# Attention and MLP in one kernel: casts placed ahead of their transposes, constants filled by block on VectorE, a rate of MLP work for each block

## The chip, the cores and the metric

The kernel runs on one core of one Trainium2 chip. The metric is the time on the device in microseconds (us), the median of several runs. A ratio is the mean time of one kernel's fast runs over that of the other's of the same rounds, so it is not quite the ratio of the medians that are quoted beside it.

The program fills the instruction queues of five engines: TensorE (PE in the profile; PEld are its weight loads), VectorE (DVE), ScalarE (ACT), GpSimd (POOL) and SyncE (SP, which here issues DMAs). The program lays down the order of each queue. Semaphores order the queues against each other.

## The reference, cut to what matters

```python
# q, k, v: 4 batches x 8 heads x 768 x 64, float32
ub     = sum_d max(q*k_min(chunk), q*k_max(chunk))    # bound for each of 24 chunks of 32 keys
sel    = the 6 chunks of the highest bound (causal)
scores = where(sel & causal, q @ k.T / 8, -1e9)
x      = softmax(scores) @ v                          # -> 3072 tokens x 512
h      = x @ w_in                                     # 512 x 2048
g      = softplus(h)
out    = g @ w_out                                    # 2048 x 512, float32
```

## The kernel before

The tokens are cut into 12 blocks of 256, in the order `00 10 01 11 02 12 20 21 30 31 22 32` (batch, block within the batch). The instructions of all engines are issued in an order that the program lays down itself. Its unit is the *slot*: one score step (two matmuls and one Exp), and after it whatever else the slot has to carry. There are 192 score steps and, after blocks 0 and 1, 12 slots that carry no scores, so 204 slots.

```python
def slot(rate):
    ...                                   # P*V steps and stores that have come due
    credit[0] += rate
    while credit[0] >= 1.0:
        credit[0] -= 1.0
        if next(mlp, "end") == "wait":    # the next x is not ready: the slot has no MLP step
            credit[0] = 0.0
    for g_ in agenda.pop(clock[0], []):   # steps that prepare later blocks
        next(g_, None)
    ...
```

The MLP is a stream of 192 steps. An h step is 8 matmuls of 256 columns and an Exp; every second one adds a Ln. A y step is 4 matmuls of 512 columns. x of a block has to be ready before its first h step.

```python
run_block(0, 0.0)
run_block(1, 0.0)
for _ in range(IDLE):                     # 12 slots of MLP alone
    slot(1.0)
for n in range(2, NB):
    run_block(n, 0.91)                    # 0.91 MLP steps for each slot
```

What is left of the stream after the last score runs alone at the end (the *tail*).

The first three blocks (the *ramp*) are prepared by half: cast to bf16 on ScalarE, transpose on TensorE, copy out of PSUM on ScalarE, in this order for one half of k or q, and only then for the next.

```python
def turn(xf, g):
    xb = half_pool.tile([128, NT, H // 2, D], BF16, name="xb")
    nc.scalar.copy(xb, xf[:, :, 4 * g:4 * g + 4])            # cast
    xT = new_xT()
    for t in range(NT):
        for p in range(2):
            nc.tensor.transpose(xT[:, t, p], xb[:, t, 2 * p:2 * p + 2, :], ident)
    return xT
# ... [cut] then nc.scalar.copy(kth or qt, xT)
```

Constants are written for a whole batch image at once, for two images (i = 0, 1):

```python
def consts(i):
    nc.gpsimd.memset(KB[i][0:32], 0.0)
    nc.vector.tensor_copy(KA[i][64:96], ohb.unsqueeze(1).to_broadcast([32, NP, S]))
    nc.vector.tensor_copy(KB[i][32:64], ohb.unsqueeze(1).to_broadcast([32, NP, S]))
    nc.vector.memset(BD[i], 0.0)
    nc.vector.memset(V[i][:, :, :, D:D + 1], 1.0)
```

Blocks 3 to 11 are prepared in fixed slots on VectorE (`prep_block`): chunk extremes, bounds, MAX8, comparison. The mask of chosen chunks (`mraw`) goes through a DMA transpose (`mt`), is copied into `qa` and `qt`, and the first score of the block waits for it.

The softmax here doesn't subtract the row's maximum and nothing guards it: scores larger than these inputs give would overflow.

Of the kernel before, what the change touches and what calls it, by code (L numbers as in the profile page):

```python
# [11 lines left out]
BF16 = mybir.dt.bfloat16  # L12
# [7 lines left out]
def kernel(  # L20
# [9 lines left out]
    nc = tc.nc  # L30
    B, H, S, D = q.shape
# [4 lines left out]
    NP = H // 2  # L36
# [6 lines left out]
    QB = 256  # L43
    NT = QB // 128
    NBLK = S // QB
    NCB = QB // CH
    order = "00 10 01 11 02 12 20 21 30 31 22 32"
    blocks = [(int(o[0]), int(o[1])) for o in order.split()]
# [12 lines left out]
    half_pool = ctx.enter_context(tc.tile_pool(name="half", bufs=2))  # L61
    pt_pool = ctx.enter_context(tc.tile_pool(name="pt", bufs=5))
    st_pool = ctx.enter_context(tc.tile_pool(name="st", bufs=4))
    x_pool = ctx.enter_context(tc.tile_pool(name="x", bufs=5))
    g_pool = ctx.enter_context(tc.tile_pool(name="g", bufs=3))
    e_pool = ctx.enter_context(tc.tile_pool(name="e", bufs=3))
    mo_pool = ctx.enter_context(tc.tile_pool(name="mo", bufs=3))
# [1 line left out]
    ps_o = ctx.enter_context(tc.tile_pool(name="ps_o", bufs=2, space=PS))  # L69
    ps_t = ctx.enter_context(tc.tile_pool(name="ps_t", bufs=1, space=PS))  # L70
    ps_h = ctx.enter_context(tc.tile_pool(name="ps_h", bufs=2, space=PS))
# [3 lines left out]
    KA = [singles.tile([128, NP, S], BF16, name=f"ka_{i}") for i in range(2)]  # L75
    KB = [singles.tile([128, NP, S], BF16, name=f"kb_{i}") for i in range(2)]
# [50 lines left out]
    ohb = singles.tile([32, S], BF16, name="ohb")  # L127
# [12 lines left out]
    for i in range(2):  # L140
        nc.vector.memset(Mraw[i], 0.0)

    def consts(i):
        nc.gpsimd.memset(KB[i][0:32], 0.0)
        nc.vector.tensor_copy(KA[i][64:96], ohb.unsqueeze(1).to_broadcast([32, NP, S]))
        nc.vector.tensor_copy(KB[i][32:64], ohb.unsqueeze(1).to_broadcast([32, NP, S]))
        nc.vector.memset(BD[i], 0.0)
        nc.vector.memset(V[i][:, :, :, D:D + 1], 1.0)

    def load_w_in():  # L150
        for kt_ in range(KDM):
            nc.gpsimd.dma_start(out=w_in_sb[:, kt_], in_=moe_w_in[kt_ * 128:(kt_ + 1) * 128, :])
            yield
# [18 lines left out]
    def spots(n):  # L172
        b, blk = blocks[n]
        return (KA[b % 2], KB[b % 2], BD[b % 2], Mraw[n % 2],
                blk, slice(blk * QB, (blk + 1) * QB))

    def extremes(n, ps, ts, kT):
        bd, blk = spots(n)[2], spots(n)[4]
        npp, ntt = ps.stop - ps.start, ts.stop - ts.start
        c0 = blk * NCB + 4 * ts.start  # L180
        kx = half_pool.tile([128, npp, 2, ntt, 4], BF16, name=f"kx{npp}")
        for m, op in ((0, ALU.max), (1, ALU.min)):
            nc.vector.tensor_reduce(kx[:, :, m].rearrange("d p t c -> d t p c"),
                                    kT.rearrange("d t p (c e) -> d t p c e", e=CH),
                                    axis=AX.X, op=op)
        sh = [128, npp * 2, 2, 4 * ntt]
        nc.vector.tensor_tensor(
            bd[:, ps, :, :, c0:c0 + 4 * ntt].rearrange("d p m h c -> d (p m) h c"),
            kx.rearrange("d p m t c -> d (p m) (t c)").unsqueeze(2).to_broadcast(sh),
            sel.unsqueeze(1).unsqueeze(3).to_broadcast(sh), op=ALU.mult)  # L190
# [29 lines left out]
    def prep_first(n):  # L220
        ka, kb, bd, mraw, blk, cs = spots(n)
        al = slice(0, NT)
        qt = qt_pool.tile([128, NT, NP, 128], BF16, name="qt")
        qa = qt_pool.tile([128, NT, NP, 128], BF16, name="qa")
        Q[n] = (qa, qt)
        kf, qf = xfs.pop(("k", n)), xfs.pop(("q", n))
        H2 = {}

        def new_xT():
            if n < 2:  # L230
                return ps_h.tile([128, NT, 2, 128], BF16, name="xT", tag="hp")
            return ps_t.tile([128, NT, 2, 128], BF16, name="xT", tag="t")

        def turn(xf, g):
            xb = half_pool.tile([128, NT, H // 2, D], BF16, name="xb")
            nc.scalar.copy(xb, xf[:, :, 4 * g:4 * g + 4])  # L236
            xT = new_xT()
            for t in range(NT):
                for p in range(2):
                    nc.tensor.transpose(xT[:, t, p], xb[:, t, 2 * p:2 * p + 2, :], ident)  # L240
            return xT

        def a_k(g):
            kT = turn(kf, g)
            H2["k", g] = kT, half_pool.tile([128, NT, 2, 128], BF16, name="kth")
            nc.scalar.copy(H2["k", g][1], kT)

        def a_q(g):
            qT = turn(qf, g)
            nc.scalar.copy(qt[:, :, 2 * g:2 * g + 2], qT)  # L250

        def b_(g):
            extremes(n, slice(2 * g, 2 * g + 2), al, H2["k", g][0])

        def c_(g):
            ps = slice(2 * g, 2 * g + 2)
            kt = H2["k", g][1]
            qpos = half_pool.tile([128, NT, 2, 128], BF16, name="qph")
            qneg = half_pool.tile([128, NT, 2, 128], BF16, name="qnh")
            nc.vector.tensor_scalar_max(qpos, qt[:, :, ps], 0.0)  # L260
            nc.vector.tensor_scalar_min(qneg, qt[:, :, ps], 0.0)
            H2["q", g] = qpos, qneg
            nc.gpsimd.tensor_copy(ka[0:64, ps, cs].rearrange("d p (t s) -> d p t s", s=128),
                                  kt[0:64].rearrange("d t p s -> d p t s"))
            nc.gpsimd.tensor_copy(qa[0:64, :, ps], qt[0:64, :, ps])
            nc.gpsimd.tensor_copy(kb[64:128, ps, cs].rearrange("d p (t s) -> d p t s", s=128),
                                  kt[64:128].rearrange("d t p s -> d p t s"))

        def d_(g):
            ps = slice(2 * g, 2 * g + 2)  # L270
            qpos, qneg = H2["q", g]
            ub = ps_t.tile([128, NT, 2, 2, NCH], F32, name="ub", tag="t")
            ub_sb = half_pool.tile([128, NT, 2, 2, NCH], F32, name="ub_sbh")
            m8 = half_pool.tile([128, NT, 2, 2, 8], F32, name="m8h")
            bounds(n, ps, al, qpos, qneg, ub, ub_sb, m8)
            choose(n, ps, al, ub_sb, m8)

        def e_(g):
            ps = slice(2 * g, 2 * g + 2)
            mT = ps_t.tile([64, NT, 2, 128], BF16, name="mTh", tag="t")  # L280
            for t in range(NT):
                for p in range(2):
                    nc.tensor.transpose(mT[:, t, p], mraw[:, t, 2 * g + p], ident)  # L283
            nc.vector.tensor_copy(qa[64:96, :, ps], mT[0:32])
            nc.scalar.copy(qt[32:64, :, ps], mT[32:64])

        return {"k": a_k, "q": a_q, "b": b_, "c": c_, "d": d_, "e": e_}

    def put_mask(n, mt):
        qa, qt = Q[n]  # L290
# [179 lines left out]
    def at(slot_no, gen):  # L470
        agenda.setdefault(slot_no, []).append(gen)
# [20 lines left out]
    def run_block(n, rate):  # L492
        assert n in Q
        for p in range(NP):
            for _ in score_step(n, p):
                slot(rate)
# [5 lines left out]
    def do(f, *args):  # L502
        f(*args)
        yield

    def hold(ap):
        nc.gpsimd.tensor_copy(gate, ap)

    def now(gen):
        for _ in gen:  # L510
            pass

    IDLE = 12
    starts = {}
# [14 lines left out]
    for n in range(3, NB):  # L529
# [12 lines left out]
        if n > 3:  # L542
            at(turns[0] - 14, queue(load_cast("k", n), load_cast("q", n)))
            at(max(turns[0] - 6, last_of(n) + 8), queue(load_cast("v", n)))

    consts(0)
    now(load_f32("v", 0, (nc.sync, nc.sync), 1))
    now(load_f32("k", 1, (nc.sync, nc.sync), 1))
# [1 line left out]
    now(load_f32("v", 1, (nc.sync, nc.sync), 1))  # L550
    xfq1 = xfs["q", 1]
    f0 = prep_first(0)
    for st in ("k0", "q0", "k1", "q1", "b0", "c0", "b1", "d0", "c1", "e0"):
        f0[st[0]](int(st[1]))

    def cast_v(n):
        for t in range(NT):
# [2 lines left out]
    f1 = prep_first(1)  # L560
    f2 = {}
# [10 lines left out]

    def stages(f, plan_):
        for slot_, names in plan_:
            for s_ in names.split():
                at(slot_, do(lambda s_=s_: f[s_[0]](int(s_[1]))))

    stages(f0, ((0, "d1"), (1, "e1")))
    at(2, do(cast_v, 0))
    at(3, do(consts, 1))  # L580
    at(4, do(hold, xfq1[0:1, 1, 7, 0:1]))
    at(4, do(lambda: now(load_w_in())))
    stages(f1, ((3, "k0"), (4, "q0"), (5, "b0 k1 q1"), (6, "c0 b1"), (7, "d0 c1 e0"),
                (9, "d1"), (10, "e1")))
    at(10, do(cast_v, 1))
    at(14, do(b2_loads))
    at(20, do(lambda: hold(xfq2[0][0:1, 1, 7, 0:1])))
    at(20, do(lambda: now(load_w_out())))
    at(20, do(lambda: now(load_cast("v", 2))))
    at(20, queue(load_cast("k", 3), load_cast("q", 3), load_cast("v", 3)))  # L590
    stages(f2, ((19, "k0"), (20, "b0"), (21, "q0 c0"), (22, "d0"), (23, "e0 k1"), (24, "b1"),
                (25, "q1 c1"), (26, "d1"), (27, "e1")))
    run_block(0, 0.0)
    run_block(1, 0.0)
    for _ in range(IDLE):
        slot(1.0)
    for n in range(2, NB):
        run_block(n, 0.91)
    while later:
        slot(1.0)  # L600
    clock[0] = NEVER
# [32 lines left out]
```

## Time and profile before

331.24 us, the median of 3 runs (330.64 to 331.49). The profiled run is another one. It took 332.4 us, so spans read from its trace exaggerate by about 1 us.

The first lines of the profile page of before: busy time with its share of the span for each engine, and two rows of the 40 slices (tenths busy of TensorE, and tenths of full speed that its clock was granted).

```profile
span 330.7 us, 6455 instructions
PE 265.0 (80%) x2472; PEld 185.8 (56%) x2472; DVE 162.8 (49%) x571; ACT 216.1 (65%) x371; POOL 112.5 (34%) x189
...
PE   1443594669877989898898699789899999999994
...
PEclk9999999778999799999999799979999999999999
```

The slices are 8.3 us long. TensorE is mostly at 8 or 9 from slice 10 on and mostly between 1 and 6 before. Holes remain (a 6 at slice 23).

The table of stretches of before, cut where the stages change: until the first MLP matmul, the slots of MLP alone, until the last Exp of attention, and the tail. The columns are start and end, length, busy us of PE, PEld, DVE, ACT and POOL with instruction counts, the mean granted clock of TensorE, the DMA share and GB/s. The clock record of these traces begins only near 46 us, so the 1.00 of a first line was not measured.

```profile
0.00:44.00 44.00, 17.65 (x151) 11.84 (x152) 28.49 (x96) 21.45 (x41) 22.06 (x41) 1.00 0.71 126
44.00:74.00 30.00, 19.46 (x148) 13.54 (x149) 9.93 (x38) 17.74 (x27) 16.15 (x23) 0.83 1.31 165
74.00:294.00 220.00, 196.40 (x1964) 141.18 (x1964) 119.69 (x430) 161.13 (x283) 73.86 (x126) 0.97 0.77 88
294.00:331.00 37.00, 31.46 (x214) 19.22 (x212) 4.67 (x8) 15.83 (x22) 0.41 (x1) 0.99 0.13 47
```

No engine is full in the first 74 us: that is a chain. From 74 us on TensorE is 89% busy, and what it leaves idle is 24 us in the long stretch.

What TensorE waited for, in two windows of before, from the view of waits (who waited for whom, us in total, number of waits, longest). First 44 to 74 us, then 74 to 294 us.

```profile
PE xT L240 <- ACT xb L236: 9.5, 4, 2.5
...
PE s_ps L348 <- ACT pt L352: 6.7, 16, 0.9
PE y L428 <- DVE y_sb L433: 5.3, 6, 1.7
PE s_ps L348 <- DVE qa L293: 5.1, 4, 3.1
PE ub L198 <- DVE qpos L308: 2.8, 2, 2.1
```

The first line is four groups of transposes that waited 2.4 us each for a cast. The cast itself takes 0.60 to 0.62 us, but it stands in ScalarE's queue behind Exp and Ln of the MLP, as the timeline of ScalarE in before shows (start, duration, engine, line, operation, tiles; idle time before it in brackets):

```profile
48.91 1.07 ACT L414 ACTIVATE e_sb<-hp 128x512 f32<-128x512 f32 x2
50.01 1.06 ACT L416 ACTIVATE g<-e_sb 128x1024 bf16<-128x1024 f32 x1
50.97 0.60 ACT L236 CAST xb<-two 128x512 bf16<-128x512 f32 x1
```

The timeline of the start of before, VectorE and POOL:

```profile
1.60 3.09 DVE L130 TENSOR_SCALAR ohb<-ident,shift 32x768 bf16<-32x768 bf16 x1
1.63 2.65 POOL L144 MEMSET kb_110<- 32x3072 bf16 x1
...
8.08 0.64 DVE L183 TENSOR_REDUCE kx_199<-xT 128x16 bf16<-128x512 bf16 x1
```

VectorE's instruction, which fills `ohb`, takes 3.09 us for 768 elements per partition. (Some texts below call it the first VectorE operation; two short ones, of 0.18 and 0.14 us, go before it.)

### The profile page before, as it was taken

The page shows a single profiled execution, that of the slowest core. Times are in us where ns is not written, and L with a number is a line of the kernel's source. Part 1 is how long each engine was busy: PE and PEld are TensorE (multiplying, and loading weights), DVE is VectorE, ACT ScalarE, POOL GpSimd, SP SyncE. Part 2 cuts the span into 40 slices and gives each one's busy share as a digit, 9 for nine tenths or more (in the row PEclk, how much of TensorE's full clock was granted, in tenths as well). Part 3 has the DMA queues.
Part 4 walks back from the last instruction along what each step waited for, and adds up shares of the span by engine and source line. Part 5 has one row for each costly group of instructions (what it writes and reads, how often), then busy time and mean ns, then how long its engine had stood idle before and what let it go on. Part 6 is the DMA issues. An engine that isn't in the chain of part 4 may idle for free.

```text
span 330.7 us, 6455 instructions
## 1 busy us (share of the span) xinstructions
PE 265.0 (80%) x2472; PEld 185.8 (56%) x2472; DVE 162.8 (49%) x571; ACT 216.1 (65%) x371; POOL 112.5 (34%) x189
## 2 busy tenths in 40 slices
PE   1443594669877989898898699789899999999994
PEld 0222363436534756765765586567567767776641
DVE  8764622433657548636756957549375211111001
ACT  4454367559534794985794599658787978876540
POOL 5357228545433422404536545732111001000000
PEclk9999999778999799999999799979999999999999
DMA  9908679999999856765999799999211110001101
GB/s 168 212 2 164 123 148 144 179 135 113 102 107 145 95 47 113 93 83 64 163 83 111 130 112 98 113 95 144 64 44 23 49 49 33 18 34 53 60 32 63
DMA packets 118082, 31.48 MB, mean 95 GB/s; under 512 B 112420, under 2 KB 114468, under 8 KB 118052
## 3 DMA queue, kind: packets, MB, share of 16 engines
q0 software_dynamic: 60928, 11.54, 43.9%
q1 hardware_dynamic: 55012, 19.01, 29.0%
q10 hardware_dynamic: 2112, 0.52, 0.9%
q8 instruction: 19, 0.31, 0.4%
q14 instruction: 11, 0.09, 0.1%
HBM read 27.26 MB, written 6.29 MB: 101 GB/s over the span
## 4 chain that ended last, share of the span: by engine, by line
PE 52%; ACT 23%; DVE 15%; DMA 5%; issue 4%; POOL 0%; ACTq 0%; POOLq 0%
PE y L428 19%; PE hp L412 18%; ACT g L416 7%; ACT e_sb L414 7%; ACT pt L352 6%; PE s_ps L348 5%; PE o_ps L373 5%; DMA mt<-mraw_115 4%; PE s_ps L350 3%; DVE y_sb L433 2%; DMA x<-o_sb 2%; ACT xb L236 1%; PE xT L240 1%; PE mTh L283 1%; DVE m8h L207 1%
## 5 line engine op out<-in xcount | busy, mean ns | idle before, releaser
L352 ACT ACTIVATE pt<-s_ps 128x512 bf16<-128x512 f32 (+1 forms) x192 | 99.4, 540 | 45.3 <-PE s_ps L350 44.2
L412 PE MATMUL hp<-x,w_in_sb 128*128 128x256 bf16 x768 | 106.3, 285 | 1.8 <-DMA x<-o_sb 1.5
L428 PE MATMUL y<-w_out_sb,g 128*128 128x512 bf16 x384 | 98.4, 381 | 6.9 <-DVE y_sb L433 6.9
L356 POOL TENSOR_SCALAR_AFFINE_SELECT pt<-pt 128x256 bf16<-128x256 bf16 x96 | 40.5, 423 | 160.2 <-ACT pt L352 159.6
L412 PEld LDWEIGHTS <-w_in_sb 128*128 128x128 bf16 x768 | 75.7, 102 | 16.5 <-issue 2.5
L414 ACT ACTIVATE e_sb<-hp 128x512 f32<-128x512 f32 x96 | 57.3, 598 | 32.7 <-PE hp L412 32.2
L428 PEld LDWEIGHTS <-g 128*128 128x128 bf16 x384 | 34.9, 98 | 34.5 <-issue 8.9
L416 ACT ACTIVATE g<-e_sb 128x1024 bf16<-128x1024 f32 x48 | 50.7, 1057 | 1.5
L379 DVE RECIPROCAL rec<-o_ps 128x4 f32<-128x4 f32 x48 | 8.8, 183 | 79.9 <-PE o_ps L373 79.9
L433 DVE COPY y_sb<-y 128x512 f32<-128x512 f32 x24 | 16.6, 690 | 42.7 <-PE y L428 42.6
L373 PEld LDWEIGHTS <-pt 128*128 128x128 bf16 x672 | 30.1, 102 | 3.3 <-issue 1.2
L240 PE MATMUL xT<-ident,xb 128*128 128x128 bf16 x48 | 6.4, 278 | 24.4 <-ACT xb L236 24.4
L383 DVE TENSOR_TENSOR o_sb<-o_ps,rec 128x256 bf16<-128x256 f32 x48 | 20.4, 424 | 1.7
L240 PEld LDWEIGHTS <-xb 128*128 128x128 bf16 x48 | 3.7, 119 | 27.5 <-ACT xb L236 27.5
L348 PE MATMUL s_ps<-qa,ka_109 96*128 96x256 bf16 x48 | 13.7, 287 | 6.3 <-DVE qa L293 3.6
L373 PE MATMUL o_ps<-v_107,pt 128*128 128x65 bf16 x336 | 17.0, 200 | 1.0 <-ACT v_107 L558 1.0
L348 PE MATMUL s_ps<-qa,ka_108 96*128 96x256 bf16 x48 | 14.1, 295 | 3.5 <-DVE qa L293 1.5
L116 POOL DMA_DIRECT2D k_sb<-in_k_dram x18 | 16.3, 906 | 1.2 <-issue 0.7
L348 PE MATMUL s_ps<-qt,kb_110 128*128 128x256 bf16 x48 | 14.0, 291 | 3.2 <-ACT pt L352 3.0
L116 POOL DMA_DIRECT2D q_sb<-in_q_dram x18 | 16.2, 901 | 0.9 <-issue 0.3
L373 PE MATMUL o_ps<-v_106,pt 128*128 128x65 bf16 x336 | 16.3, 198 | 0.0
L348 PE MATMUL s_ps<-qt,kb_111 128*128 128x256 bf16 x48 | 13.8, 289 | 1.0 <-ACT pt L352 0.7
(190 smaller groups left out, 319.0 us busy)
## 6 DMA issues: line engine op xcount, KB each, us to landing
out_dram<-y_sb SPq DMA_DIRECT2D x24, 256.0 KB, 2.0
k_sb<-in_k_dram POOLq DMA_DIRECT2D x18, 128.0 KB, 4.1
q_sb<-in_q_dram POOLq DMA_DIRECT2D x18, 128.0 KB, 4.6
w_in_sb<-in_moe_w_in_dram POOLq DMA_DIRECT2D x4, 512.0 KB, 8.2
w_out_sb<-in_moe_w_out_dram POOLq DMA_DIRECT2D x4, 512.0 KB, 9.6
v_106<-in_v_dram POOLq DMA_DIRECT2D x10, 128.0 KB, 5.5
v_107<-in_v_dram POOLq DMA_DIRECT2D x10, 128.0 KB, 4.8
two<-in_v_dram SPq DMA_DIRECT2D x4, 256.0 KB, 5.2
```

What stands on the lines that cost most here:

```text
L116: nc.gpsimd.dma_start(out=xb[:, t], in_=rows(nm, n, t))
L240: nc.tensor.transpose(xT[:, t, p], xb[:, t, 2 * p:2 * p + 2, :], ident)
L348: nc.tensor.matmul(s_ps[:, 0:QB], kk[0:nr, p, j * 128:(j + 1) * 128], qq[0:nr, :, p, :], start=True, stop=True)
L352: nc.scalar.activation(pt[:, h, j:j + 2].rearrange("k j c -> k (j c)")[:, 0:w], s_ps[:, 0:w], ACT.Exp, scale=scale)
L356: nc.gpsimd.affine_select(out=diag, in_=diag, compare_op=ALU.is_ge, fill=0.0, base=0, channel_multiplier=-1, pattern=[[0, 2], [1, 128]])
L373: nc.tensor.matmul(o_ps[:, u, h], pt[:, h, j, c0:c0 + 128], V[b % 2][:, j, 2 * p + h, :], start=(j == 0), stop=(j == t0 + u))
L383: nc.vector.tensor_tensor(o_sb[:, :, p % 2], o_ps[:, :, :, 0:D], rec.to_broadcast([128, NT, 2, D]), op=ALU.mult)
L412: nc.tensor.matmul(hp[:, fi], w_in_sb[:, dt, ft * 128:(ft + 1) * 128], X[n][:, dt // 2, :, dt % 2, :], start=(dt == 0), stop=(dt == KDM - 1))
L414: nc.scalar.activation(e_sb[:, f2 * 2:f2 * 2 + 2], hp, ACT.Exp)
L416: nc.scalar.activation(g[:, f4 * 4:(f4 + 1) * 4], e_sb, ACT.Ln, bias=1.0)
L428: nc.tensor.matmul(y, g[:, f, u * 128:(u + 1) * 128], w_out_sb[:, f, :], start=(f == 0), stop=(f == KFF - 1))
L433: nc.vector.tensor_copy(y_sb, y)
```

## The change

The intent has three parts. (1) In the ramp, casts are issued ahead of the transposes that they feed, so that TensorE and ScalarE do not take turns; one q cast of block 0 moves to VectorE, and the q transposes of blocks 0 and 1 go to other PSUM buffers than the k transposes. Loading of w_in is released two slots earlier. (2) The constants are filled for one block at a time, with the zeros on VectorE rather than on POOL. (3) The MLP gets a rate for each block: fewer steps where x is late, one for each slot from block 7 on. The number of x buffers falls from 5 to 4.

```diff
-    x_pool = ctx.enter_context(tc.tile_pool(name="x", bufs=5))
+    x_pool = ctx.enter_context(tc.tile_pool(name="x", bufs=4))
...
-    def consts(i):
-        nc.gpsimd.memset(KB[i][0:32], 0.0)
-        nc.vector.tensor_copy(KA[i][64:96], ohb.unsqueeze(1).to_broadcast([32, NP, S]))
-        nc.vector.tensor_copy(KB[i][32:64], ohb.unsqueeze(1).to_broadcast([32, NP, S]))
+    for i in range(2):
         nc.vector.memset(BD[i], 0.0)
         nc.vector.memset(V[i][:, :, :, D:D + 1], 1.0)
+
+    def consts(n):
+        b, blk = blocks[n]
+        c = slice(blk * QB, (blk + 1) * QB)
+        row = ohb[:, c].unsqueeze(1).to_broadcast([32, NP, QB])
+        nc.vector.tensor_copy(KA[b % 2][64:96, :, c], row)
+        nc.vector.tensor_copy(KB[b % 2][32:64, :, c], row)
+        nc.vector.memset(KB[b % 2][0:32, :, c], 0.0)
...   # turn() and a_k(), a_q() are split into cast (c or v), turn (t) and evac (e)
-    for st in ("k0", "q0", "k1", "q1", "b0", "c0", "b1", "d0", "c1", "e0"):
-        f0[st[0]](int(st[1]))
+    steps(f0, "ck0 vq0 tk0 tq0 ek0 eq0 ck1 cq1 tk1 tq1 b0 c0 ek1 eq1 d0 e0 b1 c1")
...
-    stages(f0, ((0, "d1"), (1, "e1")))
+    stages(f0, ((0, "d1"), (2, "e1")))
...
-    at(4, do(hold, xfq1[0:1, 1, 7, 0:1]))
-    at(4, do(lambda: now(load_w_in())))
-    stages(f1, ((3, "k0"), (4, "q0"), (5, "b0 k1 q1"), (6, "c0 b1"), (7, "d0 c1 e0"),
-                (9, "d1"), (10, "e1")))
-    at(10, do(cast_v, 1))
+    at(2, do(hold, xfq1[0:1, 1, 7, 0:1]))
+    at(2, do(lambda: now(load_w_in())))
+    stages(f1, ((3, "ck0 cq0 tk0 tq0 ek0 eq0"), (5, "ck1 cq1 b0 tk1 tq1"), (6, "c0 ek1 eq1 d0 b1"),
+                (7, "e0 c1 d1"), (9, "e1")))
+    at(9, do(cast_v, 1))
...
+    at(18, do(consts, 2))
...
-    stages(f2, ((19, "k0"), (20, "b0"), (21, "q0 c0"), (22, "d0"), (23, "e0 k1"), (24, "b1"),
-                (25, "q1 c1"), (26, "d1"), (27, "e1")))
+    stages(f2, ((19, "ck0 tk0 ek0"), (20, "b0 cq0"), (21, "tq0 eq0 c0"), (22, "d0"), (23, "e0 ck1 tk1 ek1"),
+                (24, "b1 cq1"), (25, "tq1 eq1 c1"), (26, "d1"), (27, "e1")))
+    for n in range(3, 2 * NBLK):
+        at(starts[n] - 6, do(consts, n))
...
-        run_block(n, 0.91)
+        run_block(n, {2: 0.4, 3: 0.55, 4: 0.85, 5: 0.65, 6: 0.7}.get(n, 1.0))
```

## The prediction

> **What bounds the kernel.** After the ramp, TensorE. The page gives PE 80% busy; the table by stretches gives 16 to 19.9 us of every 20 us from 80 us on. In the timeline an MLP step (8 matmuls of 256 columns, or 4 of 512) occupies PE for 0.86 to 0.88 us, a score pair for 0.17 to 0.22 us. 192 MLP steps, 192 score steps, P·V (672 matmuls at about 0.03 us) and small matmuls make some 230 us of PE work. The span is 330.7 us: about 37 us are lost before the first MLP matmul (44.2 us), 17 us from 44 to 74 us (12 MLP steps in 30 us), 30 us from 74 to 294 us, the rest at the end.
>
> The first 44 us are a chain of waits across VectorE, ScalarE and PE: ohb (3.09 us), constants (0.95 and 1.27 us), reductions (0.68 us each), MAX8, masks. POOL spends 2.65 us twice on zeros. From 44 to 74 us PE waits four times, 2.3 to 2.5 us each (9.5 us in the waits), for a ScalarE cast (0.62 us) queued behind Exp and Ln of the MLP.
>
> **What the change does.**
> 1. Constants by block. Whole-image copies become thirds, about 0.33 us each, plus a zero memset, estimated at 0.2 to 0.6 us from the 0.27 us of the 256-element uint32 memset (the Trainium skill, "VectorE: DVE Perf Modes", Zero memsets can be issued as uint32; the trace names uint32 there). About 1 us leaves VectorE before block 0, another 1 us within the ramp; POOL loses 5.3 us. Later blocks pay about 1.2 us of VectorE each, mostly hidden.
> 2. Casts first. On blocks 0 and 1 PE and ScalarE alternate less. For block 2 the q casts go one slot ahead, the k casts do not: two of the four waits go. One q cast moves to VectorE behind the constants, which gives back block 0's gain: first score about 14.5 us, as now (14.6).
> 3. Weights start two slots earlier; they landed at 37.7 us, not binding.
> 4. With the trace's durations laid out in engine order, the first MLP matmul comes at about 42.5 us, the first score of block 2 at about 70 us (74.0). **Ramp: −4 us.**
> 5. Rates move steps, they remove none: block 2 does 6 instead of 14, blocks 7, 10, 11 more (16, 24, 24 for 10, 22, 22). By the order counted from the code, 28 steps remain after the last score in both, so the tail (37 us) stays. The gain is in the holes: slots 50–54, 90–95 and 113–120 had no MLP step while x, the mask transposes (5 to 6.7 us) or VectorE were awaited. I take 8 of the 30 us back. Block 2 itself runs about 7 us shorter but owes 8 steps (6.9 us). Mask latency (one slot of 4.5 us near 212 us) stays.
> 6. x buffers 5→4: nothing.
>
> **Total:** 331 − 4 − 8 = **319 us**, range 311 to 326. Chances: faster 0.80, same 0.18, slower 0.02.
>
> **What would show it.** First MLP matmul near 42.5 us; two, not four, waits for casts between 44 and 70; first score of block 2 near 70; PE idle from there to the last score down from 22–25 to about 15 us; tail 37 us; PE busy still about 265 us.
>
> **What would make it wrong.** VectorE preparing block 3 may bind block 2 once its slots are short, so that the deferred steps cost their full time; half-clock time in a thinner block 2; masks landing later than shorter slots allow.

## The result, and the profile after

314.74 us, the median of 3 runs (313.77 to 316.79), against 331.24 us. The ratio is 0.9516, with a 95% interval from 0.9439 to 0.9594. So the kernel is faster, by 16.5 us; the prediction had 12 us.

The same lines of the page of after. The slices are 7.8 us long here.

```profile
span 313.0 us, 6470 instructions
PE 256.8 (82%) x2472; PEld 182.8 (58%) x2472; DVE 164.8 (53%) x586; ACT 216.4 (69%) x370; POOL 107.8 (34%) x187
...
PE   1344495566868799998889999999999999999984
...
PEclk9999999899879999999999999999999999999999
```

The same 2472 matmuls were busy for 8.2 us less. From slice 13 on the clock row has no dip, and from slice 22 to slice 38 TensorE is at 9 throughout.

The table of stretches of after, cut at the same stages:

```profile
0.00:42.00 42.00, 17.06 (x149) 11.38 (x149) 26.05 (x99) 20.93 (x39) 16.65 (x39) 1.00 0.73 132
42.00:70.00 28.00, 18.22 (x153) 13.48 (x152) 11.94 (x42) 18.35 (x28) 16.47 (x23) 0.94 1.33 166
70.00:276.00 206.00, 189.70 (x1959) 138.50 (x1958) 122.12 (x439) 160.94 (x281) 74.28 (x126) 0.98 0.93 95
276.00:313.00 37.00, 31.79 (x217) 19.44 (x215) 4.66 (x8) 16.16 (x23) 0.41 (x1) 0.99 0.13 47
```

The tail is the same 37 us. The ramp is 4 us shorter, the long stretch 14 us: 7 us less idle and 7 us less busy for work that is the same but for a few instructions at the edges.

The waits of TensorE in after, from 42 to 70 us and then from 70 to 276 us:

```profile
PE xT L253 <- ACT xbk L238: 4.1, 2, 2.3
PE ub L203 <- DVE qph L271: 2.5, 2, 1.4
...
PE xT L253 <- ACT xbq L238: 0.3, 1, 0.3
...
PE s_ps L363 <- ACT pt L367: 8.3, 9, 1.6
PE s_ps L363 <- DVE qa L308: 5.1, 4, 3.1
PE ub L203 <- DVE qpos L323: 1.5, 2, 1.0
```

Two waits for a k cast stay and the two for a q cast are gone, as foretold. The waits of y for its copy on VectorE (5.3 us in before) are gone from the long stretch.

The timeline of the start of after:

```profile
1.59 0.61 DVE L130 TENSOR_SCALAR ohb<-ident,shift 32x768 bf16<-32x768 bf16 x1
...
4.92 0.48 DVE L153 MEMSET kb_110<- 32x512 uint32 x1
...
6.18 1.29 DVE L188 TENSOR_REDUCE kx_198<-xT 128x16 bf16<-128x512 bf16 x2 [0.29 <-ACT kth L259]
...
9.01 0.62 ACT L238 CAST xbq<-two 128x512 bf16<-128x512 f32 x1 [1.31 <-DMA two<-in_q_dram]
```

The `ohb` operation now takes 0.61 us, not 3.09. VectorE reaches its first reduction 1.9 us earlier. The first score comes only 0.8 us earlier (13.8 for 14.6 us), because the last q half of block 0 lands at 9.0 us and its cast waits for it.

**How the numbers of the next table are read from the traces.** "Block 2" is the start of the first score matmul of block 2. "Middle" goes from there to the start of the last Exp. "Idle" is TensorE's idle time within the middle. "Half" is how much of the middle lay in stretches that the trace's clock record gives as 0.5. These stretches are 3.4, 6.8 or 10.2 us long, but for a last one that the end of the record cuts. The times are those of the profiled run of each kernel.

| profiled run | span | block 2 | middle | idle | half | tail |
|---|---|---|---|---|---|---|
| before | 330.7 | 74.0 | 219.7 | 23.6 | 13.6 | 37.0 |
| after | 313.0 | 69.6 | 206.5 | 16.3 | 6.8 | 37.0 |
| e1_rates_only | 326.8 | 74.4 | 215.4 | 22.5 | 20.3 | 37.0 |
| e2_ramp_only | 323.5 | 70.5 | 216.1 | 26.0 | 3.4 | 37.0 |
| e3_filled_holes | 327.3 | 74.8 | 215.5 | 20.1 | 0.3 | 37.0 |
| e4_consts_only | 330.9 | 73.7 | 220.2 | 24.8 | 16.7 | 37.0 |
| e5_rates_early | 324.5 | 73.8 | 206.6 | 20.8 | 13.7 | 44.1 |
| e6_rates_late | 326.6 | 74.7 | 220.5 | 19.0 | 10.3 | 31.5 |
| e7_pool_zeros | 317.1 | 70.9 | 209.2 | 18.0 | 10.2 | 37.0 |
| e8_k_casts_ahead (slow) | 316.0 | 69.0 | 210.0 | 18.1 | 12.9 | 37.0 |
| e9_warm_rates_only | 319.0 | 73.3 | 208.7 | 18.5 | 3.4 | 37.0 |
| e10_warm_after | 312.0 | 70.8 | 204.2 | 15.8 | 0.0 | 37.0 |
| e11_warm_k_casts | 311.5 | 67.6 | 206.9 | 15.7 | 6.8 | 37.0 |
| e12_after_again | 314.8 | 70.0 | 207.8 | 19.7 | 7.6 | 37.0 |

In e3, e9, e10 and e11 spare matmuls count as busy, so their idle time is not to be compared with the others'. The traces of e1, e2, e4 and e12 lack records: 2438 or 2444 matmuls where the kernel has 2472 (in e3, e9, e10 and e11 28 to 34 are missing too). The missing ones are matmuls of y, 24 to 30 of them in the middle, and their time counts as idle. At 0.22 us each this is an estimated 5 to 7 us, so the idle times of these rows are too high. The rows of before, after and e5 to e8 are complete.

### The profile page after: what moved, and what is told of

It is laid out like the page before. It is cut to its first block, busy times and chain, and to the rows that moved or that the text cites. A ratio compares the mean times of both kernels' runs of the same rounds, so it can differ in the third digit from the quotient of the medians.

```text
span 313.0 us, 6470 instructions
## 1 busy us (share of the span) xinstructions
PE 256.8 (82%) x2472; PEld 182.8 (58%) x2472; DVE 164.8 (53%) x586; ACT 216.4 (69%) x370; POOL 107.8 (34%) x187
## 4 chain that ended last, share of the span: by engine, by line
PE 65%; DVE 12%; ACT 12%; DMA 6%; issue 4%; ACTq 0%; DVEq 0%
PE hp L427 24%; PE y L443 21%; PE s_ps L363 6%; PE o_ps L388 6%; PE s_ps L365 4%; ACT e_sb L429 3%; ACT g L431 3%; ACT pt L367 3%; DMA two<-in_q_dram 2%; DVE m8h L212 2%; DMA mt<-mraw_115 1%; DMA mt<-mraw_114 1%; PE ub L204 1%; DMA two<-in_k_dram 1%; DVE o_sb L398 1%
## 5 line engine op out<-in xcount | busy, mean ns | idle before, releaser
L367 ACT ACTIVATE pt<-s_ps 128x512 bf16<-128x512 f32 (+1 forms) x192 | 97.9, 539 | 29.9 <-PE s_ps L365 29.1
L427 PE MATMUL hp<-x,w_in_sb 128*128 128x256 bf16 x768 | 103.3, 280 | 0.0
L427 PEld LDWEIGHTS <-w_in_sb 128*128 128x128 bf16 x768 | 74.7, 100 | 12.9
L443 PEld LDWEIGHTS <-g 128*128 128x128 bf16 x384 | 34.7, 98 | 28.5 <-issue 2.8
L363 PE MATMUL s_ps<-qa,ka_109 96*128 96x256 bf16 x48 | 13.5, 285 | 8.4 <-DVE qa L308 3.3
L363 PE MATMUL s_ps<-qt,kb_110 128*128 128x256 bf16 x48 | 13.5, 282 | 3.9 <-ACT pt L367 3.5
L388 PE MATMUL o_ps<-v_106,pt 128*128 128x65 bf16 x336 | 16.5, 199 | 0.0
L388 PE MATMUL o_ps<-v_107,pt 128*128 128x65 bf16 x336 | 16.3, 197 | 0.0
L253 PE MATMUL xT<-ident,xbk 128*128 128x128 bf16 x24 | 3.4, 292 | 14.2 <-ACT xbk L238 14.2
L363 PE MATMUL s_ps<-qt,kb_111 128*128 128x256 bf16 x48 | 13.8, 287 | 0.3
L365 PE MATMUL s_ps<-qt,kb_111 128*128 128x128 bf16 (+1 forms) x48 | 12.4, 258 | 0.0
```

Source lines behind the costliest of these rows:

```text
L363: nc.tensor.matmul(s_ps[:, 0:QB], kk[0:nr, p, j * 128:(j + 1) * 128], qq[0:nr, :, p, :], start=True, stop=True)
L365: nc.tensor.matmul(s_ps[:, QB:w], kk[0:nr, p, (j + 1) * 128:(j + 2) * 128], qq[0:nr, 1 if last else 0:, p, :], start=True, stop=True)
L367: nc.scalar.activation(pt[:, h, j:j + 2].rearrange("k j c -> k (j c)")[:, 0:w], s_ps[:, 0:w], ACT.Exp, scale=scale)
L388: nc.tensor.matmul(o_ps[:, u, h], pt[:, h, j, c0:c0 + 128], V[b % 2][:, j, 2 * p + h, :], start=(j == 0), stop=(j == t0 + u))
L427: nc.tensor.matmul(hp[:, fi], w_in_sb[:, dt, ft * 128:(ft + 1) * 128], X[n][:, dt // 2, :, dt % 2, :], start=(dt == 0), stop=(dt == KDM - 1))
L443: nc.tensor.matmul(y, g[:, f, u * 128:(u + 1) * 128], w_out_sb[:, f, :], start=(f == 0), stop=(f == KFF - 1))
```

## The experiments

The first theory was the one of the prediction, sharpened: the ramp gives 4 us and the rates the rest, each by itself, because the rates put MLP steps into holes (theory H). All kernels gave the right result. A median stands beside the median of the kernel before in the same rounds on the same chip.

### e1_rates_only: the rates alone

```diff
 # kernel before
-        run_block(n, 0.91)
+        run_block(n, {2: 0.4, 3: 0.55, 4: 0.85, 5: 0.65, 6: 0.7}.get(n, 1.0))
```

> The kernel before with only the new rates. Theory H (holes: the rates put MLP steps into stretches where TensorE idled, whatever the ramp does): the stretch from the first score of block 2 to the last Exp goes from 219.7 us to about 207, the total to about 318.5 us, the tail stays 37 us, the first score of block 2 stays at 74 us. Rival R (the middle gains because the constants and casts changed, the rates alone do little): total above 326 us.

Measured: 328.04 us (before 331.04), ratio 0.9908, interval 0.9878 to 0.9938. Three us, not 12.5. Theory H as stated falls. Two lines of the trace say where to look. The clock row of its page, and the table of stretches from 44 to 104 us:

```profile
PEclk9999999575977999999999999689999999999999
...
44.00:74.00 30.00, 19.58 (x143) 13.44 (x141) 9.72 (x38) 17.08 (x27) 15.48 (x23) 0.78 1.29 162
74.00:104.00 30.00, 21.61 (x177) 14.46 (x179) 14.33 (x51) 17.59 (x32) 13.93 (x22) 0.77 1.13 95
```

The granted clock is 0.77 from 74 to 104 us. Over the same 30 us before has 0.94. 20.3 us of the middle ran at half clock, 6.7 us more than in before. Blocks 4 to 7 and 10 and 11 took the same time as in after, within 0.1 us each (block 4: 26.5 and 26.5 us, block 7: 19.0 and 19.0). The loss against after is in the start (4.8 us), in blocks 2 and 3 (3.2 us) and in blocks 8 and 9 (5.7 us), where the first score of block 9 waits for its mask and a half-clock stretch of 6.8 us follows.

### e2_ramp_only: everything but the rates

```diff
 # kernel after
-        run_block(n, {2: 0.4, 3: 0.55, 4: 0.85, 5: 0.65, 6: 0.7}.get(n, 1.0))
+        run_block(n, 0.91)
```

> The kernel after with the old rate of 0.91 for every block. Theory H: only the ramp's gain is left, first score of block 2 near 69.6 us, middle back near 219 us, total about 326.5 us. Rival R: middle stays near 207 us, total below 319 us.

Measured: 325.49 us (before 331.04), ratio 0.985, interval 0.9816 to 0.9884. The ramp's 5.5 us is near what theory H had. But 3.0 and 5.5 make 8.5 us, and both together make 16.5 us. Eight us appear only when both are there (6.6 us by the profiled spans). Neither H nor its rival R says why.

The profiled runs say where. Add up the times from first score to first score (block 11: to the last Exp) for groups of blocks, and compare what both parts give together with the sum of what each gives alone:

| us | before | e1 (rates) | e2 (ramp) | after | together beyond the sum |
|---|---|---|---|---|---|
| start of block 2 | 74.0 | 74.4 | 70.5 | 69.6 | -1.3 |
| blocks 2 and 3 | 42.5 | 41.0 | 42.4 | 37.8 | -3.1 |
| blocks 8 and 9 | 33.1 | 34.7 | 30.4 | 29.0 | -3.0 |
| blocks 4 to 7, 10 and 11 | 144.1 | 139.6 | 143.2 | 139.6 | +0.9 |

In most blocks the rates do alone what they do in after. What the parts give only together sits in three places, and these are the places where e1 runs at half clock: from 57 to 67, from 71 to 81 and from 95 to 102, and from 207 to 214 us.

For blocks 8 and 9 this does not show an interplay of ramp and rates. In the profiled runs of e3, e4, e5 and e6, all without the new casts, the two blocks took 29.3 to 30.3 us. Only before, e1 and e9 lie above 31 us; in their traces block 9 waits longest for its mask (below). So 3.0 of the 6.6 us go with that late mask, not with the ramp.

### e3_filled_holes: spare matmuls where the MLP stream waits

```diff
 # kernel before
             if next(mlp, "end") == "wait":
                 credit[0] = 0.0
+                keep_busy()      # [helper cut] 8 matmuls w_in_sb x w_in_sb, 256 columns, into an hp tile that nobody reads
```

> The kernel before, which at each of the 9 slots where the MLP stream has to wait issues 8 matmuls of 256 columns whose result nobody reads (the output stays right). It takes no hole away, it only keeps TensorE busy in them. Theory C (clock: the holes cost because TensorE's clock halves after them; middle 13.6 us at half clock before, 6.8 after): the half-clock windows at 108 and 187 us vanish and 3 to 5 us are gained, total 326 to 328 us. Theory H: at most one window of half clock goes, total 330 to 333 us, since the work that could fill the holes is still done later.

Measured: 328.97 us (before 331.04), ratio 0.9937, interval 0.9914 to 0.996. The half-clock part of the middle fell from 13.6 to 0.3 us in the profiled run, and 2.1 us were gained. Theory C had 3 to 5 us, theory H at most 1. The run lies between the two. Half clock after these holes costs something, but taking nearly all of it out of the middle gave 2.1 us of the 16.5, so it is not the whole of what the holes cost. The test was not quite clean: before block 2 the same run had 13.4 us at half clock, where before had 10.3.

### e4_consts_only: the constants alone

```diff
 # kernel before: consts(i) replaced by consts(n) of the kernel after; BD and V filled at the start
+    at(18, do(consts, 2))
+    for n in range(3, 2 * NBLK):
+        at(starts[n] - 6, do(consts, n))
```

> The kernel before with only the constants filled block by block on VectorE. Theory P (the 3.09 us of the first VectorE operation, ohb, were a wait for the SBUF port that POOL's 2.65 us zero fill held): ohb takes 0.6 us as in the kernel after. Rival (ohb got shorter because of something else in the change, such as the casts): it stays near 3 us. First score of block 0 at most 1 us earlier than 14.6 us, because the second half of q lands at 9.1 us; first score of block 2 about 72 us, so total about 329 us, same as before within 2%.

Measured: 332.72 us (before 331.04), ratio 1.0063, interval 1.0041 to 1.0085. Block 2 started at 73.7 us, 0.3 us earlier than before, not the 2 us expected. Once block 2 ran, it took 25.4 us for 22.8. In its trace the constants of block 3 stand on VectorE from 90.9 to 92.6 us, ahead of a copy of y for which TensorE waits 3.0 us, and a half-clock stretch of 6.8 us begins at 93.7 us. On their own, the constants cost 1.7 us. But the `ohb` operation of this run is short:

```profile
1.58 0.61 DVE L130 TENSOR_SCALAR ohb<-ident,shift 32x768 bf16<-32x768 bf16 x1
```

No cast was touched here, so theory P stands and its rival falls; e7 turns it round.

### e5_rates_early and e6_rates_late: the rates in two halves

```diff
 # kernel before, e5
-        run_block(n, 0.91)
+        run_block(n, {2: 0.4, 3: 0.55, 4: 0.85, 5: 0.65, 6: 0.7}.get(n, 0.91))
 # kernel before, e6
+        run_block(n, 0.91 if n < 7 else 1.0)
```

> The kernel before with the new rates for blocks 2 to 6 and the old 0.91 from block 7 on. Theory H: nearly the whole gain of the rates, middle shorter by about 20 us but some 8 steps (6.9 us) more in the tail, total 318 to 321 us. Theory L (the full rate from block 7 on is what gains): total above 327 us.

> The kernel before with 0.91 up to block 6 and 1.0 from block 7 on. Theory H: the early holes stay, the late blocks only move steps out of the tail; total 327 to 332 us, same as before within 2%. Theory L: total 319 to 323 us.

Measured: e5 326.36 us (before 331.11), ratio 0.9865, interval 0.9829 to 0.9901; e6 328.59 us, ratio 0.9922, interval 0.9882 to 0.9961. Theory L falls: the full rate of the late blocks alone gives 2.5 us, and most of what it shows is work moved out of the tail (31.5 us for 37.0). The early rates give 4.8 us, which is less than theory H wanted: its middle is 13.1 us shorter, not 20, and its tail 7.1 us longer. As in e1, the start of its middle ran at half clock, from 70.4 to 80.6 us and from 94.3 to 101.1 us. Both halves together (e1) gave 3.0 us, less than the early half alone. In the profiled runs this shows in blocks 8 and 9: 29.3 us in e5, 29.7 in e6, 34.7 in e1.

### e7_pool_zeros: the zeros on POOL again

```diff
 # kernel after
     def consts(n):
         b, blk = blocks[n]
         c = slice(blk * QB, (blk + 1) * QB)
+        if n < 2:
+            nc.gpsimd.memset(KB[n][0:32], 0.0)
         ...
-        nc.vector.memset(KB[b % 2][0:32, :, c], 0.0)
```

> The kernel after, with the zeros of the k image filled whole on POOL again (2.65 us, twice), everything else as after. Theory P: ohb takes 3.0 us again and the first reduction of block 0 starts about 2 us later, but the first score of block 0 moves by under 1 us since it waits for the late half of q (9.0 us) and its casts; total within 1 us of after. If the port is not the cause: ohb stays at 0.61 us.

Measured: 317.6 us (before 331.11), ratio 0.9583, interval 0.9543 to 0.9623. The timeline of its start, VectorE and POOL:

```profile
1.60 3.08 DVE L130 TENSOR_SCALAR ohb<-ident,shift 32x768 bf16<-32x768 bf16 x1
1.62 2.65 POOL L151 MEMSET kb<- 32x3072 bf16 x1
...
7.72 0.68 DVE L189 TENSOR_REDUCE kx<-xT 128x16 bf16<-128x512 bf16 x1
```

With POOL's memset back (VectorE's own zero fills, which come after `ohb`, are gone), the same VectorE operation takes 3.08 us again. It ends 0.4 us after the memset does. With e4 this makes the cause shown: a zero fill on POOL held VectorE up for 2.5 us. The Trainium skill, "SBUF — State Buffer", section "SBUF: two separate sides", says that VectorE and GpSimd share a port pair under an exclusive lock, held for the whole instruction, and that the loser blocks fully. It limits this to some VectorE instructions: those in a mode that uses both ports, or with two SBUF inputs beside a GpSimd instruction that reads SBUF. The durations in these four kernels agree with a lock, but no run shows in which mode `ohb` ran. Two things stand beside it. By the trace `ohb` begins 0.03 us before the memset, and yet it is the one that waits. And not every VectorE instruction waits: beside before's second fill, from 21.5 to 24.1 us, a product took 0.43 us and a reduction 0.68 us, as elsewhere. The first score moved by 0.6 us (14.4 for 13.8). The time lies 2.9 us above the first measurement of after and 1.3 us above the second, on other chips; what it costs in the end is not resolved beyond that. The expectation had it within 1 us of after.

### e8_k_casts_ahead: the casts that the change left behind

```diff
 # kernel after
-    stages(f2, ((19, "ck0 tk0 ek0"), (20, "b0 cq0"), (21, "tq0 eq0 c0"), (22, "d0"), (23, "e0 ck1 tk1 ek1"),
+    stages(f2, ((18, "ck0"), (19, "tk0 ek0"), (20, "b0 cq0"), (21, "tq0 eq0 c0 ck1"), (22, "d0"), (23, "e0 tk1 ek1"),
```

> The kernel after, with the two k casts of block 2 issued one or two slots before their transposes, as its q casts are. My reading of the ramp (each cast behind Exp and Ln costs TensorE about 2 us): the two waits for a cast between 42 and 70 us go (2.3 and 1.8 us now), first score of block 2 at about 66 us, total about 311 us. Rival (the stretch is one chain over ScalarE, VectorE and TensorE in which casts are only a part): under 1.5 us gained.

Measured: 315.51 us (before 331.11), ratio of the fast runs 0.949, interval 0.9417 to 0.9564. The profiled run, at 317.68 us, was marked slow, as it is over 1.5% above the fastest, so its trace is used only for what TensorE waited for. The three fast runs took 315.61, 315.41 and 311.32 us, at a mean granted clock of 0.965, 0.973 and 0.989. Inconclusive on the casts by itself: in the trace the waits for the k casts fell from 4.1 to 0.8 us, but two transposes now waited 1.7 us for the copy of the mask and 1.3 us for a reduction. That looks like one chain, as the rival said. e11 tries it again. What this run gave was something else: the same program at 311 or 316 us, in the order of its clock.

### What the clock costs, from all runs

Every run records its span and its mean granted clock. Call span times (1 - clock) the *lost clock*. A least-squares fit over 84 runs of all these kernels, with a constant for each kernel and one common slope, gives 0.52 us of time for each us of lost clock, with a residual of 0.8 us (0.50 us without the one slow run, of e8; 0.58 us from the 50 runs before the last four experiments). This is an association within kernels, not yet a cause.

| mean over the runs | lost clock, us |
|---|---|
| before | 11.2 |
| e1_rates_only | 16.3 |
| e2_ramp_only | 6.6 |
| after (3 runs), e12_after_again (6 runs) | 6.3, 8.8 |

So a new theory K: the rates do fill holes, but a rate of 0.4 thins out block 2, right behind a ramp in which TensorE also idles, and its clock is halved more often. The ramp part of the change packs that stretch more tightly. The last four kernels test it by putting spare matmuls there.

### e9_warm_rates_only: is it the clock?

```diff
 # kernel e1_rates_only   # [cut] the tile y gets the same tag, "y"
+    def keep_busy(n_mm):
+        spare = ps_y.tile([128, d_model], F32, name="spare", tag="y")
+        for i in range(n_mm):
+            nc.tensor.matmul(spare[:, 0:QB], w_in_sb[:, i % KDM, 0:128], w_in_sb[:, i % KDM, 256:256 + QB],
+                             start=(i == 0), stop=(i == n_mm - 1))
     # in slot(), between the MLP step and the preparing steps
+        if 17 <= clock[0] < 28:
+            keep_busy(6)
+        elif 28 <= clock[0] < 40 and not stepped:
+            keep_busy(4)
```

> The kernel with only the new rates, which lost 16.3 us of granted clock (span times one minus the mean clock) where before lost 11.2 and after 6.3, and got 3 us instead of the 12.5 us that theory H foresaw. It gets spare matmuls of 256 columns whose result nobody reads: 6 in each slot from the second of the MLP-only stretch on, 4 in each slot without an MLP step up to slot 39. New theory K (the rates do fill holes, worth some 6 us at equal clock, but they thin out block 2, so that TensorE's clock halves more often; the ramp change made that good): lost clock falls to 8 us or less and the time to about 322 us. Rival M (the shortfall has another cause, such as late masks in blocks 8 and 9; spare work only costs time): time stays at 328 us or grows.

Measured: 319.73 us (before 331.11), ratio 0.9657, interval 0.9612 to 0.9701. Against e1 it does more work and is 8.3 us faster. Lost clock fell from 16.3 to 2.1 us. The clock row and the same stretches:

```profile
PEclk9999999999989999999999999999999999999999
...
44.00:74.00 30.00, 22.46 (x218) 18.29 (x216) 10.50 (x40) 18.86 (x29) 16.35 (x24) 1.00 1.34 166
74.00:104.00 30.00, 23.52 (x243) 16.86 (x244) 17.79 (x67) 17.79 (x34) 13.54 (x22) 0.94 1.31 111
```

The granted clock went from 0.78 and 0.77 to 1.00 and 0.94. Rival M falls, and K holds: it foresaw a gain of 6 us, and 8.3 came. Blocks 2 and 3 take 37.7 us now, for 41.0 in e1 and 37.8 in after, so there the clock was most of what the rates lacked on the old ramp. The other fast profiled runs with the new rates agree, whatever their ramp: in order of the time at half clock within blocks 2 and 3 (0, 3.4, 6.8, 6.8, 7.6, 10.2, 13.5 and 13.7 us in e10, e9, after, e11, e12, e7, e1 and e5), the two blocks took 35.6, 37.7, 37.8, 38.2, 38.3, 39.5, 41.0 and 40.9 us. That it is the new ramp which keeps the clock up is shown less well. Within these blocks the runs with both parts and no spare work (after, e7, e12) had 6.8 to 10.2 us at half clock, less than e1 and e5; but ahead of block 2, e2, e7 and e12 had 10.2 to 12.9 us on the new ramp, no less than before (10.3).

Not all of the 8.3 us can be put down to the spare work. Of the 7.8 us between the two profiled runs, the start and blocks 2 and 3 make 4.4, and blocks 8 and 9 make 3.4. Blocks 8 and 9 take 31.3 us, for 34.7 in e1 and 29.0 in after. The spare matmuls end at slot 39; the half-clock stretch at 207 us is gone in this run too, but nothing shows that the spare work, so much earlier, brought that about.

How much of the 11.4 us against before is rates and how much is clock? By the fit, the spans without lost clock would be 323.6 us for before, 317.5 for e1 and 317.2 for e9. That makes 6 us for the rates. The rest is clock that before lost as well. Before with spare matmuls in the ramp was not run, so this split is an estimate.

Of the 6.0 us by which the profiled run of after is still ahead of it (319.0 and 313.0), 3.7 us are the start of block 2 (73.3 and 69.6 us). 2.3 us are block 8 (11.9 and 9.6 us), where this kernel, like before and e1, waits for the mask of block 9 and after does not.

### e10_warm_after, e11_warm_k_casts, e12_after_again: the same on the kernel after

The edits are the `keep_busy` lines of e9 on the kernel after (e10) and on e8 (e11). e12 is the kernel after, unchanged, on the same chip.

> The kernel after with the same spare matmuls. After lost 6.3 us of clock on average, of which some 4 us lie between 55 and 95 us. Theory K: lost clock falls to about 3 us, time about 312.5 us (after: 314.7), with less spread between runs. Rival M: time at 316 us or more, since the spare matmuls stand in front of transposes in TensorE's order.

> The kernel with the k casts of block 2 ahead, whose four runs went from 311.3 us at a granted clock of 0.989 to 317.7 us at 0.962, with the same spare matmuls. Theory K: all runs near the fast end, about 311 us. Rival M: median stays at 315 us or above.

> The kernel after once more, beside the others on the same chip. About 314.7 us; the runs should order by granted clock, with about 0.6 us of time for each us of lost clock.

Measured, all against 331.11 us of before:

| kernel | median, us | range | ratio (95% interval) | lost clock, us |
|---|---|---|---|---|
| e12_after_again | 316.31 | 315.84 to 317.85 | 0.9555 (0.9524 to 0.9586) | 8.8 |
| e10_warm_after | 314.51 | 313.73 to 317.64 | 0.9518 (0.9475 to 0.956) | 3.2 |
| e11_warm_k_casts | 313.25 | 311.12 to 313.56 | 0.9443 (0.9411 to 0.9475) | 2.7 |

e10 lost as little clock as K foresaw, but was 2 us slower than expected, its spread did not shrink, and its interval overlaps that of after. The spare matmuls stand in front of the transposes in TensorE's queue: block 2 started at 70.8 us for 70.0. So on the kernel after, the spare work pays back little more than it takes. e11 is faster than after on the same chip: the intervals are apart, and 0.9443 over 0.9555 makes 1.2%. It beats both kernels, by 2 us less than expected of it. Against e10 it is 1.3 us faster at the median and 2.5 us by the mean, and the two intervals touch. So what the k casts are worth, and whether it is under 1.5 us as the rival of e8 said, is not resolved. e12 was 1.6 us above the first measurement of after, on another chip, and lost more clock. Its runs did not order strictly by clock (315.90 us at 0.966, 317.38 us at 0.966), so the clock is not all of the scatter.

## Why the prediction was right or wrong

**The total.** 319 us was predicted, 311 to 326 us the range; 314.74 us was measured. Faster by over 2% had a chance of 0.80 and came.

**The ramp, -4 us: right.** First MLP matmul 42.3 us (predicted 42.5), first score of block 2 at 69.6 us (70), two of four waits for casts gone, first score of block 0 at 13.8 us (14.5). By itself the ramp part measured 5.5 us.

**Its reasons were partly wrong.** The prediction counted the constants as less VectorE work. It took the 3.09 us of the `ohb` operation as its length, though 768 elements per partition cannot explain it beside the 0.95 us that a copy of 3072 took in the same trace. Most of it was a wait for POOL's memset, which the change removes (e4, e7). That this hardly moved the time is because another wait took its place: the q load that lands at 9.0 us. The constants alone cost 1.7 us (e4), so the ramp's gain must come from the casts and from how they go together with the rest. The casts alone were not run. How much of it the earlier release of w_in has was not tried; it lands at 32.6 us for 37.7, both well before it is used.

**The rates, "I take 8 of the 30 us back": the mis-sized term.** In the traces the middle is 13.2 us shorter. 7.3 us of it is idle time (23.6 to 16.3 us, predicted about 15), so the holes were sized well. The other 5.9 us are busy time, and the line of the prediction that failed is "PE busy still about 265 us": it was 256.8 us. The time at half clock within the middle fell from 13.6 to 6.8 us, which can make up to 3.4 us of it. Another part lies in how busy time is counted. A score matmul followed at once by another counts 0.11 us, one followed by idle time its whole bar of 0.27 us. At full clock 17 score matmuls of the middle were followed by idle time in before and 7 in after, which makes an estimated 1.6 us. The remaining 0.9 us or more were not traced. The prediction named half clock only as a risk of a thinner block 2, not as a cost that before already paid and that denser work would end.

**The sum, "331 - 4 - 8": wrong as a sum.** It adds two terms as if each stood alone. Alone they are 5.5 and 3.0 us, together 16.5 us. On the old ramp the rates are a small gain. They thin out block 2 there and lose clock (e1), and giving the clock back went with 8.3 us (e9), of which 3.4 us lie in blocks 8 and 9. So the two errors partly cancelled: by themselves the rates give less than the 8 us of the prediction, and with the new ramp they give more (325.49 us in e2 for 314.74 in after, on different chips). That the total came out near was in part luck.

**"Block 2 itself runs about 7 us shorter": wrong.** From first score to first score it went from 22.8 to 19.6 us. The risk named at the end came true. The timeline of TensorE in after, at its last score and the first of block 3:

```profile
85.49 0.58 PE L388 MATMUL o_ps<-v_106,pt 128*128 128x65 bf16 x14
89.21 0.28 PE L363 MATMUL s_ps<-qa,ka_109 96*128 96x256 bf16 x1 [3.13 <-DVE qa L308]
```

VectorE finished the comparison at 84.1 us, the mask transpose took from 84.2 to 88.8 us, and only then could block 3 start. From the first score of block 2 to the issue of this transpose it took 14.6 us (17.3 in before), and the transpose another 4.6 (5.1). The chain shrank by 3.2 us, not by 7.

**"Mask latency (one slot of 4.5 us near 212 us) stays": wrong.** From its last score of block 8 to the first of block 9, before took 4.47 us:

```profile
216.15 0.28 PE L348 MATMUL s_ps<-qa,ka_109 96*128 96x256 bf16 x1 [3.10 <-DVE qa L293]
```

The same slot took 1.56 us in after. In before that transpose took 6.7 us from issue to landing, in e1 4.9 and in after 3.2 us. Why is not settled: no run isolated it. With the old rates the slot took 1.92 to 2.55 us in e2, e3, e4 and e6, so the rates are not its cause alone.

**Right:** the tail (37.0 us in both), the x buffers (no wait for one is seen), the two k casts that stay exposed.

## What to carry to other kernels

Two parts of a change can be worth little alone and more together when one of them thins out TensorE's work and the other packs it, so try each part by itself before naming its worth. When busy time changes with the work unchanged, look at the granted clock: filling a hole can buy the half-clock stretch behind it as well, and moving work out of a dense stretch may lose more clock than it gains. Count the matmul records of two traces before their idle times are compared. An instruction that takes five times as long as in another run of the same size may be waiting inside its own bar, so look for what another engine started at the same moment.

## What the Trainium skill lacked or had wrong

- "TensorE: Matmul & The Clock Gate", Part 1, gives two clock states, full and half, and windows of about 3.4 us. The traces agree: every dip that ends within the record is given as 0.5 and is 3.4, 6.8 or 10.2 us long, and 256-column matmuls follow each other at 0.109 us outside the dips and at 0.213 us within (medians of before and after). The same part says that, for modelling, the penalty of the ramp at the start is under 1% of a typical kernel's span. That figure is not for dips later in a kernel, which cost more here: e9, with the clock kept up, was 8.3 us faster than e1, 2.5% of its span, though not all of this is the clock's.
- The same page advises against idle gaps of TensorE. It has nothing on spare matmuls within a kernel as a measure; here the kernel with them was 8.3 us faster in one case (e9), 2.1 us in another (e3) and not clearly in a third (e10).
- "SBUF — State Buffer", "SBUF: two separate sides", has a shared lock of VectorE and GpSimd, which fits the runs, though by the trace `ohb` began first (by 0.03 us) and waited. It does not say how that looks in a profile: the 2.5 us of waiting stood inside the bar of the VectorE instruction (3.09 for 0.61 us).
- "VectorE: DVE Perf Modes", "Zero memsets can be issued as uint32", agrees: the zero fill of 1024 bf16 elements per partition appears as 512 uint32 elements and took 0.48 us.
- No page says that the clock record of a trace can begin late: here it starts at 46.6 us in before (46.2 in after) and the profile shows 1.00 up to there, while the first twelve MLP matmuls of before, from 44.2 to 46.5 us, follow each other at 0.20 to 0.21 us, as in the dips.
